# A long-convolution and feed-forward kernel on one core: one transform step, 32-row taps, one filter sum by accumulating transfers, and new orders

## The chip, the cores and the metric

The kernel runs on one core of a Trainium2 chip. The metric is the device time of one execution in microseconds, 258.08 us in the middle of three runs (257.58 to 259.14). All five engines of the core take part: TensorE (PE in the profile; its weight loads are PEld) multiplies, VectorE (DVE) and ScalarE (ACT) do elementwise work and empty PSUM, GpSimd (POOL) computes small powers and issues accumulating transfers, SyncE (SP) issues the other transfers.

## The reference

The reference has two halves. In the first, the layer-normed input q gates a long causal convolution: k is shifted by four taps, multiplied by v, convolved along the sequence (2048 tokens, 640 channels) with a filter as long as the sequence, and added to the input. The second is a gated feed-forward block on the layer-normed sum.

```python
k_shift = k_shift + k_pad[:, t:t + S, :] * shift_k[:, ks - 1 - t][None, None, :]   # t in range(4)
kv = k_shift * v
y = irfft(rfft(kv padded to 2S) * rfft(ssm_k padded to 2S))[:S] + kv * ssm_D
h = x + _layernorm(x) * y
h2 = h + (silu(_layernorm(h) @ w_gate) * (_layernorm(h) @ w_up)) @ w_down
```

## The kernel before

The sequence is cut into four blocks of 512 tokens. The convolution is done per block in a frequency space of 512 points: signal block j is transformed to XH (a "signal transform", xfwd), filter block m to a spectrum (kfwd), block i of the output is the sum over j of products of signal j with a combined filter C[i-j] (prod), and the inverse transform (inverse) gives block i back, followed by the residual, the second layer norm and the transposed store into hnT for the feed-forward step (ffn). The line `SEQ` fixes the order in which these steps enter the graph: signal block 1 (S1), products into output block 1 (P11), inverse 1 (I1), feed-forward of block 0 (F0) and so on.

Every operation is a task with a name, added by `g.add` with the engine it may run on and what it reads and writes. `PLAN` holds one hand-fixed order of task numbers per engine (pe, act, dve, pool, sp) and one string `units`, which gives each PSUM tile one of four units of two banks. Each engine runs its list strictly in order. `arrange` (L135) adds the waits: a task that opens a PSUM tile waits for the users of the tile that had that unit before. So an engine that has to wait holds back all that stands behind it in its list.

Names that the text uses: `ktM.P` transposes filter block M for the even or odd half, `kfM.fpc` transforms it (L588) and `kbM` are its sums and differences, `kteM.P` and `kfMe...` the copies out of PSUM; `kcM` or `kcomb(M)` adds neighbouring filter spectra (L677); `tpI.c` are the tap matmuls of block I from channel chunk c on (L738), `keI.c` their copies out of PSUM, `kvI.c` the multiplication by v (L745); `xfI...` the signal transform (L625 or L588), `xbI.n` its sums on VectorE; `pJI.ff` the products (L780); `ybI` and `ivI` the inverse; `fgI`, `fuI` gate and up matmuls (L1032), `muI` their product, `dnI` the down matmuls (L1118); `laI` the first layer norm.

The tap step (L722 to L747) is a set of small matmuls: for each chunk of 128 channels and each of 7 offsets, one matmul per group of 64 channels, with K = 64 rows and 256, 192, 128, 64, 192, 128 or 64 columns. It multiplies a shifted slice of k by a block-diagonal tap matrix. So a chunk takes 14 matmuls of 7 steps, two side by side on the two halves of the array, and a block's five chunks 70 matmuls in three tasks with a PSUM tile each.

The signal transform has three forms. `fulls` (L593) does all by matmuls. `halves` (L574) splits the tokens into even and odd, takes 8 groups of 4 matmuls of 320 columns, and adds and subtracts the halves on VectorE (two operations of 2560 elements per partition). `quads` (L611) splits twice, takes 8 groups of 2 matmuls, and needs four operations of 1280 and two of 2560 on VectorE. Before, blocks 1, 2 and 3 use `quads` (`R4X`). Filter transforms use `halves`.

`kcomb(2)` adds filter spectrum 2 onto spectrum 1 by one VectorE operation of 5120 elements (L687); `kcomb(3)` does it with two accumulating transfers that POOL issues (L680, `addto`, L570).

Of the kernel before, what the change touches and what calls it, by code (L numbers as in the profile page):

```python
# [12 lines left out]
P = 128  # L13
# [37 lines left out]
class _Graph:  # L51
# [41 lines left out]
    def add(self, name, engs, fn, kind, r=(), w=(), pr=(), pw=(), skip=(), dma=False):  # L93
# [4 lines left out]
        t.opens = None  # L98
# [18 lines left out]
        for pt in pw:  # L117
            if not pt.writers:
                t.opens = pt
# [15 lines left out]
    def arrange(self, plan):  # L135
# [19 lines left out]
        for t in self.order["pe"]:  # L155
            if t.opens is not None:
                prev = last.get(t.opens.unit)
                if prev is not None:
                    t.pre = {x for x in prev.users if x.eng != "pe"}
                    t.deps.update(t.pre)  # L160
                last[t.opens.unit] = t.opens
# [21 lines left out]
    def emit(self, block):  # L183
# [29 lines left out]
        for t in self.glob:  # L213
            kn = known[t.eng]
            fill = self.fills.get(t.name)
            if fill:
                wait_for(t, t.pre | {x for x in t.deps if x.name == fill[0]})
                prog["pe"].append(lambda e, t=t, fill=fill: self.filler(e, t.opens, *fill))
# [50 lines left out]
    "act":  # L269
# [10 lines left out]
    "dve":  # L280
# [10 lines left out]
    "pool":  # L291
        "19 17 15 16 125 165 174 158 192 183 223 225 224 342 396 362 281 371 285 401 380 289 406 389 343 293 420 415 527 466 "
        "470 561 474 552 478 579 570 684 586 591 529 705 710 698 637 732 723 641 645 750 649 741 "
        "",
    "sp":
        "0 2 3 8 4 6 10 7 230 9 11 13 14 235 296 226 12 229 297 227 481 231 167 176 228 234 295 233 194 185 482 232 364 282 373 "
        "290 391 294 286 382 480 653 652 471 563 554 467 475 479 581 572 651 734 725 638 752 646 743 642 650 798 807 801 804 "
        "810 "
        "",
    "units":  # L300
        "0131203132312001201201213230032110213023012230313133033220021021122013200230230222110332013110130232003210332301202110"
        "01310112312301210312031012210230131023033303012010313012013"
        "",
# [7 lines left out]
def bass_sequential_preLN__ssm_conv_h3__swiglu_ffn__prompt_kernel(  # L311
# [30 lines left out]
    SA = ()  # L342
    DA = ((1,2),(1,3),(2,3),(3,3))
    KD = (3,)
    DD = (2,)
    LO = (('k',2),('k',3),('x',3))
# [3 lines left out]
    JP = (0,1)  # L350
    SEQ = "P01 K W F0 S1 P11 I1 P02 P12 P03 P13 F1 S2 P22 I2 P23 F2 S3 P33 I3 F3"
# [5 lines left out]
    BNH = ()  # L357
# [4 lines left out]
    R4X = (1,2,3)  # L362
# [19 lines left out]
    with ExitStack() as es:  # L382
# [29 lines left out]
        KO = sb("KO", 143616, [2, 2, D])  # L412
# [246 lines left out]
        def kfwd(m, dst):  # L659
            if m in R4K:  # L660
                quads("kf%d" % m, KT[m], dst, KO, D ** 0.5 / N, m)
                return
# [3 lines left out]
            halves("kf%d" % m, KT[m], dst, KO, D ** 0.5 / N, m)  # L666
            if ("k", m) in LO:
                bfly("kb%d" % m, dst[:, 0:2], KO[:], dst[:, 0:2], dst[:, 2:4], 4 * D, part=1)
                addto("kb%d.1" % m, dst[:, 0:2], KO[:])
                return  # L670
            if ("k", m) in MB:
                bfly("kb%d" % m, dst[:, 0:2], KO[:], dst[:, 0:2], dst[:, 2:4], 4 * D)
                return
            for f in range(2):
                bfly("kb%d.%d" % (m, f), dst[:, f], KO[:, f], dst[:, f], dst[:, f + 2], 2 * D)

# [22 lines left out]
        def taps(i):  # L699
# [22 lines left out]
            for c0 in (0, 2, 4):  # L722
                nc_ = min(2, NC5 - c0)
                pt = g.tile()
# [504 lines left out]
```

## Time and profile before

| what | value |
|---|---|
| timed runs | 257.58, 258.08, 259.14 us; median 258.08 us |
| span of the profiled execution | 256.0 us (no other time is given for that execution) |
| median less span | 2.1 us |
| PE, DVE, ACT, POOL busy in the span | 97%, 78%, 72%, 23% |
| granted TensorE clock | 1.000 |

The span runs from the first to the last instruction. A matmul's end is modelled: its busy time includes the drain, so rows of 320-column matmuls show a mean of 300 ns, while a long run of them starts one every 136 ns. The cost of a matmul on PE is therefore read from the start of one group to the start of the next.

### The profile page before, as it was taken

How to read it: one execution, taken by the hardware profiler on the slowest of the kernel's cores; microseconds unless marked ns; L12 is line 12 of the kernel's file. 1: busy time of each engine (PE TensorE's matmuls, PEld its weight loads, DVE VectorE, ACT ScalarE, POOL GpSimd, SP SyncE). 2: the span in 40 equal slices, each digit the busy share in tenths (PEclk: the TensorE clock that was granted, in tenths of full speed). 3: DMA queues.
4: the chain of work that ended last, by engine and by line, in shares of the span. 5: the costliest groups of instructions: out<-in, count | busy, mean ns of one | idle time of the engine just before them, and what ended most of it. 6: DMA issues, size and time to landing. Idle time of an engine off the chain costs nothing.

```text
span 256.0 us, 5303 instructions
## 1 busy us (share of the span) xinstructions
PE 248.5 (97%) x2253; PEld 194.7 (76%) x2253; DVE 199.8 (78%) x256; ACT 184.6 (72%) x302; POOL 58.6 (23%) x56
## 2 busy tenths in 40 slices
PE   7999997999999999999999999999999999999995
PEld 4767773587888766888887766788886678888763
DVE  3698999999999999999999989999959534111142
ACT  2489999999996895587899789739981854526410
POOL 1001003082312053950030813334130314000000
PEclk9999999999999999999999999999999999999999
DMA  6999946787995049886956036497870142600011
GB/s 224 323 339 208 403 161 134 220 207 192 326 188 95 0 75 126 150 165 168 248 100 109 3 55 139 108 213 139 149 128 0 30 100 43 140 0 3 0 45 57
DMA packets 37620, 35.29 MB, mean 138 GB/s; under 512 B 21203, under 2 KB 32478, under 8 KB 37598
## 3 DMA queue, kind: packets, MB, share of 16 engines
q1 hardware_dynamic: 31792, 23.82, 33.2%
q0 software_dynamic: 5792, 11.14, 25.3%
q8 instruction: 17, 0.28, 0.4%
q14 instruction: 5, 0.04, 0.1%
q10 hardware_dynamic: 14, 0.01, 0.0%
HBM read 16.55 MB, written 2.62 MB: 75 GB/s over the span
## 4 chain that ended last, share of the span: by engine, by line
PE 59%; DVE 32%; DMA 4%; POOL 1%; SPq 1%; issue 1%; ACT 0%; DVEq 0%
PE ps L1032 32%; PE ps L1118 16%; DVE tt L780 9%; DVE Y L780 5%; DMA tab<-cst_tab 4%; PE ps L602 3%; PE ps L922 2%; DVE gu L1053 2%; DVE C L780 2%; DVE XH L637 2%; DVE C L564 2%; PE ps L995 2%; PE ps L622 2%; PE ps L584 2%; POOL mv L840 1%; SPq L450 1%
## 5 line engine op out<-in xcount | busy, mean ns | idle before, releaser
L1118 PE MATMUL ps<-Wd,gu 128*128 128x320 bf16 (+1 forms) x420 | 58.7, 300 | 0.0
L1118 PEld LDWEIGHTS ps<-Wd,gu 128*128 128x128 bf16 (+1 forms) x420 | 38.7, 97 | 18.4 <-issue 3.6
L780 DVE TENSOR_TENSOR tt<-XH,C 128x2560 bf16<-128x2560 bf16 (+1 forms) x31 | 47.8, 1572 | 0.6 <-ACT XH L458 0.6
L1053 DVE TENSOR_TENSOR gu<-gu,ub 128x1024 bf16<-128x1024 bf16 (+1 forms) x32 | 19.9, 621 | 26.4 <-ACT gu L1040 13.8
L1040 ACT ACTIVATE gu<-ps 128x1024 bf16<-128x1024 f32 (+1 forms) x32 | 29.4, 924 | 12.1 <-PE ps L1032 11.9
L1045 ACT ACTIVATE ub<-ps 128x1024 bf16<-128x1024 f32 x24 | 24.6, 1024 | 13.3 <-PE ps L1032 11.4
L1032 PE MATMUL ps<-hnT,GB 128*128 128x256 bf16 x280 | 34.0, 273 | 0.0
L1032 PE MATMUL ps<-hnT,UB 128*128 128x256 bf16 x280 | 33.8, 273 | 0.0
L1032 PEld LDWEIGHTS ps<-hnT,UB 128*128 128x128 bf16 x280 | 27.3, 98 | 3.4 <-ACT KO L458 0.2
L1032 PEld LDWEIGHTS ps<-hnT,GB 128*128 128x128 bf16 x280 | 27.2, 98 | 3.3
L1032 PE MATMUL ps<-hnT,GA 128*128 128x256 bf16 x240 | 28.8, 273 | 0.0
L1032 PE MATMUL ps<-hnT,UA 128*128 128x256 bf16 x240 | 28.5, 273 | 0.1
L840 POOL TENSOR_TENSOR mv<-mv,half 128x1 f32<-128x1 f32 x16 | 21.2, 1328 | 23.9 <-DVE mv L838 23.9
L1032 PEld LDWEIGHTS ps<-hnT,UA 128*128 128x128 bf16 x240 | 23.4, 98 | 3.4 <-ACT C L458 0.5
L1032 PEld LDWEIGHTS ps<-hnT,GA 128*128 128x128 bf16 x240 | 23.4, 98 | 3.2 <-DVE XH L461 0.3
L843 ACT ACTIVATE qo<-xh 128x640 bf16<-128x640 bf16 x28 | 21.0, 750 | 5.8 <-DMA xh<-in_A_q_dram 3.3
L584 PE MATMUL ps<-KT,tab 128*128 128x320 bf16 x128 | 19.8, 300 | 1.8 <-ACT K3r L458 0.7
L937 ACT ACTIVATE qo<-ps,one,st 128x640 bf16<-128x640 f32 x16 | 13.7, 887 | 9.8 <-PE ps L922 9.0
L571 POOL DMA_DIRECT2D xh<-RB x12 | 10.7, 889 | 34.4 <-DVE RB L1135 23.0
L584 PEld LDWEIGHTS ps<-KT,tab 128*128 128x128 bf16 x128 | 11.4, 98 | 8.6 <-ACT K3r L458 1.6
L840 POOL TENSOR_TENSOR st<-st,half 128x4 f32<-128x4 f32 x4 | 8.0, 1988 | 33.3 <-DVE st L835 21.5
L458 ACT ACTIVATE XH<-ps 128x640 bf16<-128x640 f32 x19 | 13.3, 736 | 1.4 <-PE ps L622 0.7
(112 smaller groups left out, 384.3 us busy)
## 6 DMA issues: line engine op xcount, KB each, us to landing
C<-US POOLq DMA_DIRECT2D x6, 640.0 KB, 6.0
kc<-in_A_ssm_k_dram SPq DMA_DIRECT2D x4, 640.0 KB, 10.3
xh<-in_A_q_dram SPq DMA_DIRECT2D x4, 640.0 KB, 5.6
out_dram<-xh SPq DMA_DIRECT2D x15, 160.0 KB, 1.9
kvo<-in_A_v_dram SPq DMA_DIRECT2D x3, 640.0 KB, 4.5
xh<-RB POOLq DMA_DIRECT2D x12, 160.0 KB, 2.9
Wd<-in_B_w_down_dram SPq DMA_DIRECT2D x1, 1280.0 KB, 7.9
C<-K3r POOLq DMA_DIRECT2D x2, 640.0 KB, 8.0
```

Source lines behind the costliest of these rows:

```text
L458: return e.activation(out=dst[1], in_=src(), func=ACTF.Copy, scale=scale)
L571: return g.add(name, "pool", lambda e, n: e.dma_start(dst, src, accum_op=ALU.add, max_dma_last_dim=4096), ("acc", 2 * int(np.prod(dst.shap ...
L584: last = e.matmul(pt.f(c, W), tab[:, f, cs, j], src[:, j, c * W:(c + 1) * W], start=(j == js[0]), stop=(j == js[1]))
L780: g.add(nm, "dve", lambda e, n_: e.tensor_tensor(out=d, in0=a, in1=b, op=op), ("sb", n * D), r=[a, b], w=[d])
L840: g.add(name + "r", "pool", lambda e, n: e.tensor_tensor(out=dst, in0=tmp, in1=hf, op=ALU.pow), ("pp", 4), r=[tmp, half[:]], w=[dst])
L843: g.add(name + "m", "act", lambda e, n: e.activation(out=junk, in_=x, func=ACTF.Identity, scale=-1.0 / D, accum_out=sm), ("aa", D, 0), r=[ ...
L937: g.add(nm + "e", "act", lambda e, n, pt=pt, q2=q2, s=s, j=j: e.activation(out=q2, in_=pt.f2(W), func=ACTF.Identity, scale=s[:, 3, j:j + 1 ...
L1032: last = e.matmul(pt.f(q // 2, 256, o=256 * (q % 2)), w[:, c, f0:f0 + P], hnT[:, c, cols], start=(c == 0), stop=(c == NC5 - 1))
L1040: g.add("sg%d.%d%d" % (i, h, gp), "act", lambda e, n, pa=pa, gv=gv, nf=nf: e.activation(out=gv, in_=pa.f(0, 256 * nf).rearrange("p (f x) - ...
L1045: g.add("su%d.%d%d" % (i, h, gp), "act", lambda e, n, pb=pb: e.activation(out=ub[:].rearrange("p b x -> p (b x)"), in_=pb.f(0, 1024), func ...
L1053: g.add("mu%d.%d%d" % (i, h, gp), "dve", lambda e, n, gv=gv, ubv=ubv: e.tensor_tensor(out=gv, in0=gv, in1=ubv, op=ALU.mult), ("sb", 256 * ...
L1118: last = e.matmul(pt.f(c, W), gu[k, fb, col(i, j)], Wd[k, fb, c * W:(c + 1) * W], start=st, stop=sp)
```

## The change

Four things change. `R4X` loses block 1, so signal block 1 is transformed by `halves` and not by `quads`. `KD` gains block 2, so `kcomb(2)` is two accumulating transfers. For blocks 1 to 3 the first four channel chunks of the taps form one task of 32-row matmuls, four side by side, which opens two PSUM tiles at once; the fifth chunk stays as it was. And all five orders and the PSUM units are new. `DV`, `KOT` and `BNT` are empty tuples, so the code that they guard adds no task; `KO` becomes four names for the same place.

```diff
-    KD = (3,)
+    KD = (2,3)
+    T32 = ((0, 4, 32), (4, 1, 64))
-    R4X = (1,2,3)
+    R4X = (2,3)
...
-            for c0 in (0, 2, 4):
-                nc_ = min(2, NC5 - c0)
-                pt = g.tile()
+            for c0, nc_, rr in T32 if i in KVACT else ((0, 2, 64), (2, 2, 64), (4, 1, 64)):
+                nr = P // rr
+                pts = [g.tile() for _ in range(nr // 2)]
...
                         for s in (0, 1, 2, 3, -1, -2, -3):
                             j0, j1 = max(0, s), min(3, 3 + s) + 1
                             k0 = 16 + s
-                            for r in range(2):
-                                rows = slice(64 * r, 64 * r + 64)
-                                last = e.matmul(pt.f(r, 64 * (j1 - j0), o=256 * b + 64 * j0), ks[rows, c, k0:k0 + 509:4], diag[rows, c, j0 - s:j1 - s, :],
-                                                start=(s == 0), stop=(s == -3))
+                            for r in range(nr):
+                                rows = slice(rr * r, rr * r + rr)
+                                x0 = rr * r % 64
+                                last = e.matmul(pts[r // 2].f(r % 2, rr * (j1 - j0), o=4 * rr * b + rr * j0), ks[rows, c, k0:k0 + 509:4],
+                                                diag[rows, c, j0 - s:j1 - s, x0:x0 + rr], start=(s == 0), stop=(s == -3),
+                                                **({"tile_position": (rr * r, 0)} if rr < 64 else {}))
...
+                    for h, pt in enumerate(pts):
+                        kh_ = kr[:, 2 * h:2 * h + 2]
+                        evac("ke%d.%d%s" % (i, c0, "ab"[h] if nr > 2 else ""), (kh_, kh_),
+                             lambda pt=pt, nc_=nc_, rr=rr: pt.f2(4 * rr * nc_).rearrange("p r (b y) -> p r b y", b=nc_), 8 * rr * nc_, pt)
+                    g.add("kv%d.%d" % (i, c0), "dve", lambda e, n, d=d, vv=vv, ks_=ks_, rr=rr, nr=nr: e.tensor_tensor(
+                        out=d.rearrange("p j (b x) -> p b j x", x=rr), in0=ks_.rearrange("p b (r j x) -> p (b r) j x", r=nr, j=4),
+                        in1=vv.rearrange("p j (b x) -> p b j x", x=rr), op=ALU.mult), ("sb", N * nc_), r=[vv, ks_], w=[d])
```

In `arrange`, `opens` becomes a list, since a tap task now opens two tiles and waits for the users of both. Per block of 1 to 3 the taps have two matmul tasks instead of three, still three copies out of PSUM (`ke.0a` and `ke.0b` of 1024 elements, `ke.4` of 512), and two multiplications by v (2048 and 512 elements) instead of three (1024, 1024, 512).

The task numbers in `PLAN` are not the same in both files, so the orders are told here by the names behind them. The parts that the prediction speaks of:

```
PE, before:  xf0(2) kf0(8) kt1 xf0(2) kt2.0 xf0.31 kt2.1 xf0(3) kf1 ... tp1.2 tp1.0 iv0.0 iv0.1 tp1.4 kf2/kf3/xf1 mixed ... fu0.00
             (first matmul of F0; xf1 last group, kt3.1 and seven groups of kf3 stand among F0)
PE, after:   xf0.00 kf0(8) xf0(3) kt1 xf0(4) kf1(5) kt2 kf1(3) kt3.0 tp1.0 tp1.4 iv0.0 iv0.1 kf2(5) kt3.1 kf2/xf1/kf3 mixed ... fg0.00
             (all of xf1 and four groups of kf3 ahead of F0)
PE, both:    ... F0 ... iv1, dn0, two groups of F1, taps of block 2, xf2, rest of F1, dn1, taps of block 3, iv2, xf3, F2, F3
DVE, after, new among the copies out of PSUM: kf0e.111 kte2.1 ke1.4 kf2e.001 kf2e.010 kte3.1 xf1e.001 (ACT before, but kf0e.111)
DVE, before, now on ACT or POOL: kf0e.011 kte0.0 lp0
DVE, before the last kv of block 2: p03.c mu1.00 kv2.2 kv2.0 kv2.4 p03.d ... iv1.3n
DVE, after:                         iv1.3n ... p03.c kv2.4 p03.d kv2.0 ... mu1.00
POOL, before: iv0.0r iv0.1r kb2.1 iv0.3r iv0.2r kb3.1 kc3.1 kc3.0 la1r
POOL, after:  iv0.0r iv0.1r lp0 kb2.1 kc2.1 iv0.2r iv0.3r kc2.0 kb3.1 kc3.1 kc3.0 lp1 la1r
SP, before:   kT1 GA itab UB v1 UA kT2 PKu ht0.0 ht0.1 GB WdC x1 WdB ht0.3 ht0.2 v2 WdA
SP, after:    kT1 itab UA v1 x1 GB PKu WdC GA UB WdB kT2 ht0.0 ht0.1 v2 ht0.2 ht0.3 WdA
```

More of the change, by code (lines that the diff above doesn't have):

```diff
@@ L97, in add @@
         t.pre = set()
-        t.opens = None
+        t.opens = []
         t.tiles = []
@@ L118, in add @@
             if not pt.writers:
-                t.opens = pt
+                t.opens.append(pt)
             else:
@@ L155, in arrange @@
         for t in self.order["pe"]:
-            if t.opens is not None:
-                prev = last.get(t.opens.unit)
+            for pt in t.opens:
+                prev = last.get(pt.unit)
                 if prev is not None:
-                    t.pre = {x for x in prev.users if x.eng != "pe"}
-                    t.deps.update(t.pre)
-                last[t.opens.unit] = t.opens
+                    t.pre |= {x for x in prev.users if x.eng != "pe"}
+                last[pt.unit] = pt
+            t.deps.update(t.pre)
         for t in self.tasks:
@@ L217, in emit @@
                 wait_for(t, t.pre | {x for x in t.deps if x.name == fill[0]})
-                prog["pe"].append(lambda e, t=t, fill=fill: self.filler(e, t.opens, *fill))
+                prog["pe"].append(lambda e, t=t, fill=fill: self.filler(e, t.opens[0], *fill))
             wait_for(t, t.deps)
@@ L356, in bass_sequential_preLN__ssm_conv_h3__swiglu_ffn__prompt_kernel @@
     BN = (0,)
-    BNH = ()
+    BNT = ()
+    KOT = ()
     DT = ()
@@ L411, in bass_sequential_preLN__ssm_conv_h3__swiglu_ffn__prompt_kernel @@
         v0 = sb("v0", 134400, [4, D])
-        KO = sb("KO", 143616, [2, 2, D])
+        KO = [sb("KO%d" % m, 174336 if m in KOT else 143616, [2, 2, D]) for m in range(4)]
         ub = sb("ub", 148736, [2, N])
@@ L742, in taps @@
                     ks_ = XT[i % 2][:, c0:c0 + nc_, :]
[L743 to L747 removed]
+                    kr = ks_.rearrange("p b (r y) -> p r b y", r=nr)
+                    for h, pt in enumerate(pts):
[5 more added lines that the diff above has]
+                        in1=vv.rearrange("p j (b x) -> p b j x", x=rr), op=ALU.mult), ("sb", N * nc_), r=[vv, ks_], w=[d])
                     continue
@@ L799, in prod @@
                 op2(nm + ".d", yim, u[:, :, 0], u[:, :, 1], ALU.add, 4)
+                return
+            if (j, i) in DV:
+                x, k, re = XH[j % 2][:], cm[:], tt[:, 1].rearrange("p a b d -> p (a b) d")
+                im = US[:].rearrange("p a b c d -> p (a b) c d")
+                ksw = bass.AP(k.tensor, k.offset + D, [list(k.ap[0]), [2 * D, 4], [-D, 2], [1, D]])
+                nm = "p%d%d" % (j, i)
+                for f2 in range(2):
+                    s = slice(f2, f2 + 3, 2)
+                    op2(nm + ".%da" % f2, t1, x[:, s], k[:, s], ALU.mult, 4)
+                    op2(nm + ".%dc" % f2, re[:, s], t1[:, :, odd], t1[:, :, 1 - odd], ALU.subtract, 2)
+                addto(nm + ".0e", y[:, :, odd], re)
+                op2(nm + ".0b", im, x, ksw, ALU.mult, 8)
+                for q in range(2):
+                    addto(nm + ".%df" % q, y[:, :, 1 - odd], im[:, :, q])
                 return
@@ L973, in inverse @@
                     stats(nm, x, q[:], m[:, 0:1], m[:, 1:2])
-                rstd(nm, m[:, 1:2], m[:, 3:4], m[:, 2:3], half[:, 0:1], i in BNH or i in SA, D ** -2.0 if i in SA else float(D))
+                rstd(nm, m[:, 1:2], m[:, 3:4], m[:, 2:3], half[:, 0:1], (i, j) in BNT or i in SA, D ** -2.0 if i in SA else float(D))
                 if i in NACT:
@@ L984, in inverse @@
                 g.add(nm + "n", "dve", lambda e, n, x=x, q=q, m=m, mm_=mm_: e.tensor_scalar(
-                    out=q[:], in0=x, scalar1=mm_, scalar2=m[:, 3:4], op0=ALU.subtract if i in BNH + SA else ALU.add, op1=ALU.mult),
+                    out=q[:], in0=x, scalar1=mm_, scalar2=m[:, 3:4], op0=ALU.subtract if (i, j) in BNT or i in SA else ALU.add, op1=ALU.mult),
                       ("ts", D), r=[x, mm_, m[:, 3:4]], w=[q[:]])
```

42 lines of the change are left out of this document (18 added, 24 removed), and 53 rows, old and new, of the table PLAN.

## The prediction

> **What bounds the kernel now.** I read the page first: the engine shares, then the slices.
>
> ```profile
> span 256.0 us, 5303 instructions
> PE 248.5 (97%) x2253; PEld 194.7 (76%) x2253; DVE 199.8 (78%) x256; ACT 184.6 (72%) x302; POOL 58.6 (23%) x56
> ...
> PE   7999997999999999999999999999999999999995
> ...
> DVE  3698999999999999999999989999959534111142
> ACT  2489999999996895587899789739981854526410
> ```
>
> PE is busy in nearly every slice. DVE is at nine tenths from the fifth slice to the twenty-fifth, ACT from the fourth to the eleventh. So two limits lie close together up to about 160 us, and PE alone remains after it. The table by stretches says how close (PE, PEld, DVE, ACT, POOL).
>
> ```profile
> core 0: us, PE busy (x) PEld busy (x) DVE busy (x) ACT busy (x) POOL busy (x), PEclk, DMA share, GB/s
> ...
> 28.20:40.50 12.30, 12.30 (x147) 9.08 (x144) 12.19 (x11) 12.30 (x21) 0.00 (x0) 1.00 0.73 245
> 40.50:49.30 8.80, 6.72 (x40) 2.81 (x40) 8.42 (x12) 8.80 (x16) 2.38 (x2) 1.00 0.56 119
> 49.30:113.20 63.90, 63.51 (x588) 51.27 (x588) 63.30 (x69) 53.60 (x92) 26.44 (x19) 1.00 0.74 161
> 113.20:161.30 48.10, 47.83 (x440) 37.39 (x440) 46.27 (x60) 41.77 (x72) 12.54 (x11) 1.00 0.53 116
> 161.30:253.40 92.10, 92.07 (x781) 74.80 (x780) 48.79 (x72) 49.43 (x81) 15.27 (x17) 1.00 0.39 78
> ```
>
> From 40.5 to 113.2 DVE works 71.72 of 72.7 us; from 161.3 on PE has 92.07 of 92.1. In 40.5 to 49.3 ACT is full (8.80 of 8.80) while PE runs only 40 matmuls. The chain of waits and PE's timeline price them (start, duration, what; a bracket holds idle time and what ended it).
>
> ```profile
> 18.68 1.12 PE ps L550 x20
> ...
> 24.18 3.27 PE ps L602 x24
> ...
> 121.58 13.10 PE ps L1032 x120
> ...
> 138.46 2.28 PE ps L734 x63
> 140.74 3.93 PE ps L1032 x35
> ```
>
> ```profile
> 14.72 3.96 PE L584 MATMUL ps<-KT,tab 128*128 128x320 bf16 x28 [0.20 <-DMA tab<-cst_tab]
> ...
> 43.29 0.45 PE L622 MATMUL ps<-kvo,tab 128*128 128x320 bf16 x2
> 43.88 0.44 PE L622 MATMUL ps<-kvo,tab 128*128 128x320 bf16 x2
> ...
> 105.78 2.35 PE L1032 MATMUL ps<-hnT,GA 128*128 128x256 bf16 x20
> 108.05 2.47 PE L734 MATMUL ps<-diag,kT 64*128 64x256 bf16 x70
> 110.45 2.36 PE L1032 MATMUL ps<-hnT,GB 128*128 128x256 bf16 x20
> 113.23 0.72 PE L622 MATMUL ps<-kvo,tab 128*128 128x320 bf16 x4 [0.42 <-DVE kvo L745]
> ...
> 159.69 1.69 PE L622 MATMUL ps<-kvo,tab 128*128 128x320 bf16 x10 [0.24 <-DVE mv L838]
> ```
>
> A 320-column matmul costs 3.27/24 = 0.136 us, so the 40 of that stretch are 5.45 us of work in 8.80: PE stands idle for 3.35 us there, waiting for ACT to empty PSUM. Two groups of the signal transform start 0.59 us apart (43.29, 43.88) for 0.27 us of matmuls. The next idle time is 0.42 us at 113.23, where signal block 2 waits for the product kv2 on DVE. Then come 0.24 us at 159.69 and, early, 0.20 us at 14.72 for a table. So PE's stalls that the change could reach are 3.35 + 0.42 + 0.24 + 0.20 = 4.2 us, and everything else is PE's own work.
>
> **The change, part by part.**
>
> *Signal block 1 by halves.* PE gets 8 groups of 4 matmuls for 8 of 2: 16 x 0.136 = +2.18 us. ACT's eight copies stay. It falls where PE waited on ACT, so part of it costs nothing as long as those stalls last; I count it in full against the removed stalls. DVE prices:
>
> ```profile
> L1053 DVE TENSOR_TENSOR gu<-gu,ub 128x1024 bf16<-128x1024 bf16 x24 | 16.5, 688 | 23.1 <-ACT gu L1040 13.8 <-ACT ub L1045 9.3
> ...
> L637 DVE TENSOR_TENSOR XH<-OS,XH 128x2560 bf16<-128x2560 bf16 x5 | 7.4, 1487 | 0.0
> L984 DVE TENSOR_SCALAR qo<-xh,mv 128x640 bf16<-128x640 bf16 x16 | 7.1, 444 | 2.7 <-POOL mv L840 2.7
> ...
> L637 DVE TENSOR_TENSOR OS<-XH,OS 128x1280 bf16<-128x1280 bf16 x6 | 4.9, 820 | 0.2 <-ACT OS L458 0.2
> ...
> L745 DVE TENSOR_TENSOR kvo<-XT,kvo 128x1024 bf16<-128x1024 bf16 x6 | 3.9, 685 | 0.0
> ...
> L687 DVE TENSOR_TENSOR C<-C,C 128x5120 bf16<-128x5120 bf16 x1 | 2.8, 2822 | 0.0
> ...
> L461 DVE TENSOR_SCALAR KO<-ps 128x640 bf16<-128x640 f32 x1 | 0.8, 825 | 0.4 <-PE ps L584 0.4
> ...
> L460 DVE COPY KT<-ps 128x1280 bf16<-128x1280 bf16 x1 | 0.8, 815 | 0.0
> ```
>
> The next start on DVE comes some 0.08 us before the modelled end (the operation at 50.65 below lasts 1.49 us and the next begins at 52.05), so an operation costs 0.08 us less than its duration. DVE loses four operations of 1280 elements and keeps two of 2560: 4 x 0.74 = -2.96 us.
>
> *Filter sum 2 by transfers.* DVE loses one operation of 5120 elements, 2.82 - 0.08: -2.74 us. POOL gets two issues and the queues two transfers of 640 KB.
>
> ```profile
> C<-K3r POOLq DMA_DIRECT2D x2, 640.0 KB, 8.0
> ...
> C<-KO POOLq DMA_DIRECT2D x1, 640.0 KB, 5.8
> ```
>
> ```profile
> 50.65 1.49 DVE L564 TENSOR_TENSOR C<-C,KO 128x2560 bf16<-128x2560 bf16 x1
> ...
> 83.08 1.49 DVE L780 TENSOR_TENSOR tt<-XH,C 128x2560 bf16<-128x2560 bf16 x1
> ```
>
> ```profile
> 52.45 1.39 POOL L571 DMA_DIRECT2D C<-KO  x1 [9.31 <-DVE C L564]
> ```
>
> ```profile
> 27.47 0.34 SPq L450 DMA_DIRECT2D kvo<-in_A_v_dram  x1
> ```
>
> The sum is needed by the first product of signal 0 with C[2], at 83.08. Its own filter is final on DVE at 50.65 + 1.49 = 52.1. Issue and landing one after another, 1.39 + 5.8 for the KO transfer and 1.39 + 8.0 for the half that waits for it, end near 69 us; 14 us of product work on DVE hide them. I take nothing; with that cover gone all lateness past 83 us would stand on DVE. Behind them on POOL stand the powers iv0.2r and iv0.3r, whose inputs DVE makes only after kb2.0, the last thing that the transfers ahead of them wait for; la1r stood behind the transfers of filter 3 before as well. On SP, GA moves behind v1 (issued at 27.47, when signal block 0 has been read), x1 and GB: with them 3.4 MB, by 245 GB/s of the stretch 28.2 to 40.5 some 14 us, near 42; F0 begins some 8 us later and the transform groups ahead of it hide it. UB is first used later, and kT2 only by the taps of block 2. I take nothing; with the cover gone it is the lateness of the last load, up to one more 8.0 us.
>
> *Taps in 32 rows.* The widths (front: 1024 columns per group of 64 channels and chunk) sum to 5 chunks x 2 x 1024 = 10240 columns a block. At 256 columns per 13.10/120 = 0.109 us one after another they would take 4.37 us; 2.28 us from start to the next start at 140.74 in the chain says that two run side by side (2.18 us, and 0.10 for 35 steps). With the change between full and half array the block costs 110.45 - 105.78 less the 2.18 us of 20 gate matmuls, 2.49 us. After: four chunks x 512 columns = 0.87, one chunk x 1024 = 0.44, 0.10 for 35 steps, 0.31 for three changes of array form as dear as the two now, and 0.11 if a 32-column step costs as much as a 64-column one (8 steps x 13.6 ns): 1.83 us, so -0.66 per block and -2.0 for three. No row shows a 32-row matmul. Best end: without the extra change and the floor, -0.87 each. Worst end: an issue limit, with weight loads and matmuls at the mean rate of now, 2.28/126 = 18 ns; 252 instructions give 4.6 us and 4.8 with the changes, +2.3 each. I take the middle row's rate since pairs plainly overlap. The task opens two PSUM units, so it waits for the users of both, and both copies must end before other groups get them.
>
> ```profile
> L458 ACT ACTIVATE XT<-ps 128x1024 bf16<-128x1024 f32 x6 | 6.1, 1064 | 0.1
> ```
>
> Where ACT is full that is no new wait, and elsewhere PE has two units left; I take nothing, bounded by one copy, 1.06 us a block.
>
> The multiplications by v become 2048 + 512 elements. From 1280 to 2560 elements DVE takes 1487 - 820 = 667 ns, 0.52 ns each, so 2048 take 0.685 + 0.53 = 1.22 us where two took 1.37, less 0.08: -0.07 us a block. If runs of 32 elements halved the rate it would be +1.2; I take -0.07, as runs of 64 show no loss (0.685 for 1024).
>
> *Orders.* Six copies out of PSUM go from ACT to DVE: kte2.1 and kte3.1 (0.82 each), kf2e twice, xf1e.001 (0.83 each) and ke1.4 (at most that): 4.96, less 6 x 0.08: +4.5 us on DVE, as much less on ACT, which lets PE run through 40.5 to 49.3. kte0.0 goes the other way, early. And the last groups of signal block 0 stand ahead of kt2.
>
> ```profile
> 28.28 2.90 DVE L780 TENSOR_TENSOR tt<-XH,C 128x2560 bf16<-128x2560 bf16 x2 [0.29 <-ACT XH L458]
> ```
>
> Here DVE waited for them. PE's work ahead of that point shrinks by kt2 (20 transposes, 1.12 us) and the table wait, with some 0.2 us of hidden ends: DVE's chain starts about 1.6 us sooner.
>
> *The sum up to signal block 2* (113.23 now). DVE: -1.6 for the start, -2.96 - 2.74 - 0.14, +4.5: -2.9. In the new order p03.d (2560 elements, 1.41 us) and iv1.3n (0.36) stand ahead of kv2 and mu1.00 (0.61) behind: +1.2. Together -1.8, to 111.4. PE alone: -0.42 - 3.35 - 0.20 + 2.18 - 2 x 0.66 = -3.1, to 110.1. DVE is later, so the gain there is 1.8 us. *Behind it* the 1.2 us come back to DVE (-2.9 by inverse 2), so PE decides: tap block 3 gives -0.66, and the stall at 159.69 gives -0.3, as the groups of signal block 3 now stand among inverse 2, dn1.3 and fg2.00. F2 and F3 are PE's work unchanged. The sum is -1.8 - 0.66 - 0.3 = -2.8: a span of 253.2.
>
> The timed median lies 2.1 us above the span; I keep that: **255.3 us**.
>
> **The rivals.**
>
> *All of PE's stalls go.* For it: ACT is relieved by 4.5 us of copies against 3.35 us of stall. Against: DVE gets these copies and is as full. PE's account: -4.2 + 2.18 - 2.0 = -4.0: 254.1 us, and 253.4 with the best price of the taps.
>
> *The gain on DVE is eaten.* The copies now stand in DVE's strict order among products, so PE waits for DVE where it waited for ACT, and the earlier start is lost at the next wait. Then DVE gains -2.96 - 2.74 - 0.14 + 4.5 + 1.2 = -0.1 by signal block 2, and PE 0.66 behind it: -0.8: 257.3 us. For it: 71.72 of 72.7 us.
>
> *32-row matmuls are limited by issue.* This ends on the other side. The block costs 4.8 us; PE's account up to signal block 2 is 110.1 + 2 x 3.0 = 116.1, +2.9, block 3 adds 2.3 and the late stall gives 0.3: +4.9, 263.0 us. It turns slower than now when a block takes over 3.2 us. For it: no row has so dense a stream. Against: pairs run together.
>
> *Each small matmul pays a floor.* With 27 ns (64 columns at 0.109/256) for each of 112 matmuls, one after another, the block is 3.0 + 0.44 + 0.4 = 3.9 us; PE is at 110.1 + 4.1 = 114.2 at signal block 2 (+1.0), and +1.4 - 0.3 behind: 260.2 us. Against: 70 matmuls in 2.28 us have only 33 ns each while their widths average 146 columns, 62 ns; so they overlap, and a floor is paid per step. The Trainium skill, "TensorEngine Tiling (Array Packing)", section "Instruction Overhead", speaks for this rival: about 60 cycles for each matmul, and no tiling from a dimension that is small already; here the widths fall to 32 to 128 columns. By that rule, taken per matmul, the taps would cost more than now; the trace does not bear it out for two tiles and shows nothing for four.
>
> *The accumulations land late.* The transfers share their engines with the weight loads (8.0 us for 640 KB already). If landing took double, C[2] would be ready near 83 us and each further us would hold DVE; two more eat what DVE gained: 258 us.
>
> **How the numbers follow.** Forecast 0.43, all stalls go 0.13, eaten 0.22, issue limit 0.13, floor 0.05, late transfers 0.04. A measurement of this kernel can tell about 1% from no change, so faster means below 255.5 us and slower above 260.7. The forecast's own range is 254.2 to 256.4; 0.33 of the 0.43 lies below 255.5, 0.10 above. Faster: 0.33 + 0.13 = 0.46. Slower: the issue limit, 0.13. Same: 0.10 + 0.22 + 0.05 + 0.04 = 0.41. The range 253.2 to 260.5 leaves out the issue limit and a little below.
>
> **What would show it.** Taps: the groups of 32-row matmuls, some 1.8 us per block from the matmul before to the one after, and four starts close together. Halves: 32 matmuls for signal block 1, no 1280-element operations of it. Filter sum: no 5120-element addition, two more transfers landed well before the first product with C[2]. Stall: PE's idle time near 40 to 50 us well under 3.35 us. Signal block 2's first matmul near 111 us. I am wrong if the tap block takes over 2.5 us, if PE's idle time in that stretch merely moves to waits on DVE's copies, or if DVE's first product of block 0 starts no sooner than now.

## The result, and the profile after

| | before | after |
|---|---|---|
| median of the timed runs | 258.42 us (22 runs, 257.26 to 260.11) | 261.07 us (22 runs, 257.76 to 268.11) |
| ratio after to before, 95% interval | | 1.0066 [1.0041, 1.0090] |
| profiled execution | span 256.0 us | 261.59 us, span 259.7 us |

The forecast was 255.3 us, with a span of 253.2 us. The runs after scatter far more than those before. The ratio leaves out the eight longest executions after (261.99 us and more, granted clock 0.981 to 0.987), and since the kernel's own idle time lowers that clock (*warm*, below), it may understate the loss a little: the plain medians stand at 261.07 / 258.42 = 1.010.

The page of the profile after, beside the one shown of before:

```profile
span 259.7 us, 5661 instructions
...
PE 249.5 (96%) x2437; PEld 196.0 (75%) x2437; DVE 194.3 (75%) x248; ACT 184.6 (71%) x301; POOL 59.9 (23%) x59
...
PE   7999999849999999999999999999999999999995
...
DVE  2699999994699999999999987799978422121232
...
PEclk9999999988999999999999999999999999999999
```

DVE does 5.5 us less (199.8 before). PE has one gap, in the eighth and ninth slices, and the granted clock falls behind it. The table by stretches (PE, PEld, DVE, ACT, POOL, then PEclk, DMA share, GB/s) and PE's timeline show the gap from near.

```profile
40.50:50.70 10.20, 10.20 (x75) 6.75 (x73) 10.20 (x13) 10.20 (x19) 4.42 (x5) 1.00 0.98 202
50.70:55.80 5.10, 0.33 (x4) 0.04 (x2) 5.10 (x5) 4.04 (x10) 3.40 (x2) 1.00 1.06 178
55.80:60.70 4.90, 4.90 (x30) 3.69 (x31) 4.90 (x6) 0.95 (x1) 2.28 (x2) 0.65 1.12 234
```

```profile
50.31 0.71 PE L581 MATMUL ps<-kvo,tab 128*128 128x320 bf16 x4
55.79 5.10 PE L1049 MATMUL ps<-hnT,GA 128*128 128x256 bf16 x30 [4.77 <-issue]
```

The 3.35 us of stalls between 40.5 and 49.3 are gone: PE is busy for all of 40.5 to 50.7. But then F0's first gate matmul (fg0.00) starts at 55.79, after 4.77 us of idle time. It reads the columns of hnT that the first two transposed stores, ht0.0 and ht0.1, fill. And its group of 30 takes 5.10 us at a granted clock of 0.65, where 3.44 us are usual (below): 1.66 more. Both together are 6.4 us, and 259.7 - 6.4 = 253.3.

Here are the issues on SP and on POOL in that stretch (start, duration of the issue), and after them the time from issue to landing of single transfers (the last number): first those issued at 45.83 and 46.53, then those at 47.16 and 47.44.

```profile
40.44 0.37 SPq L447 DMA_DIRECT2D Wd<-in_B_w_down_dram  x1
40.85 4.94 SPq L450 DMA_TRANSPOSE kT<-in_A_k_dram  x1
45.83 1.28 SPq L450 DMA_TRANSPOSE hnT<-qo  x1
47.16 1.28 SPq L450 DMA_TRANSPOSE hnT<-qo  x1
```

```profile
46.53 1.41 POOL L568 DMA_DIRECT2D C<-KO  x1 [0.27 <-DVE C L561]
47.44 1.75 POOL L568 DMA_DIRECT2D C<-C  x1
```

```profile
C<-KO POOLq DMA_DIRECT2D x1, 640.0 KB, 9.0
hnT<-qo SPq DMA_TRANSPOSE x1, 2.7
```

```profile
C<-C POOLq DMA_DIRECT2D x1, 640.0 KB, 12.9
hnT<-qo SPq DMA_TRANSPOSE x1, 8.5
```

ht0.0 lands at 45.83 + 2.7 = 48.5. ht0.1, issued 0.63 us after C<-KO, lands at 47.16 + 8.5 = 55.7, just after C<-KO (46.53 + 9.0 = 55.5), and fg0.00 starts 0.1 us later. The profile writes "issue" beside the idle time, since it found no releaser; the landing is the one that fits. In the kernel before both stores took 2.6 us, and C<-KO was issued long after them, at 52.45. Its issues of kT2 and of the two stores, and their landing:

```profile
37.19 2.77 SPq L453 DMA_TRANSPOSE kT<-in_A_k_dram  x1
...
43.13 2.96 SPq L453 DMA_TRANSPOSE hnT<-qo  x2
```

```profile
hnT<-qo SPq DMA_TRANSPOSE x2, 2.6
```

The other steps of the change are seen in the timelines of PE and DVE:

```profile
111.03 1.88 PE L732 MATMUL ps<-diag,kT 32*128 32x128 bf16 x126
...
117.49 0.71 PE L619 MATMUL ps<-kvo,tab 128*128 128x320 bf16 x4
...
140.62 1.30 PE L732 MATMUL ps<-diag,kT 32*128 32x128 bf16 x112
```

```profile
26.98 1.49 DVE L783 TENSOR_TENSOR tt<-XH,C 128x2560 bf16<-128x2560 bf16 x1 [0.15 <-ACT XH L455]
```

A tap block takes 1.88 us (2.47 before). DVE's first product of that group starts at 26.98 (28.28 before). Signal block 2's first matmul starts at 117.49; less the 6.4 us it would be 111.1.

### The profile page after: what moved, and what is told of

Read it like the earlier page. It is cut to its first block, busy times and chain, and to the rows that moved or that the text cites. A ratio compares the mean times of both kernels' runs of the same rounds, so it can differ in the third digit from the quotient of the medians.

```text
span 259.7 us, 5661 instructions
## 1 busy us (share of the span) xinstructions
PE 249.5 (96%) x2437; PEld 196.0 (75%) x2437; DVE 194.3 (75%) x248; ACT 184.6 (71%) x301; POOL 59.9 (23%) x59
## 4 chain that ended last, share of the span: by engine, by line
PE 83%; ACT 8%; DMA 5%; DVE 1%; issue 1%; SPq 0%
PE ps L1049 45%; PE ps L1135 19%; PE ps L581 4%; PE ps L599 3%; DMA xh<-RB 3%; PE ps L944 3%; PE ps L732 2%; PE ps L939 2%; PE ps L1012 2%; DMA k0n<-in_A_k_dram 2%; PE ps L619 1%; ACT qo L862 1%; ACT qo L860 1%; PE ps L547 1%; ACT qo L954 1%; ACT RB L1151 1%
## 5 line engine op out<-in xcount | busy, mean ns | idle before, releaser
L1135 PEld LDWEIGHTS ps<-Wd,gu 128*128 128x128 bf16 (+1 forms) x420 | 38.8, 97 | 18.3 <-issue 3.5
L1049 PE MATMUL ps<-hnT,GA 128*128 128x256 bf16 x240 | 30.2, 282 | 5.0 <-issue 4.8
L1049 PEld LDWEIGHTS ps<-hnT,GA 128*128 128x128 bf16 x240 | 24.0, 101 | 9.5 <-ACT qo L862 5.1
L857 POOL TENSOR_TENSOR mv<-mv,half 128x1 f32<-128x1 f32 x16 | 19.2, 1204 | 50.7 <-DVE mv L855 50.6
L568 POOL DMA_DIRECT2D xh<-RB x12 | 11.8, 981 | 53.0 <-ACT RB L1151 53.0
L1151 ACT ACTIVATE RB<-ps,st 128x640 bf16<-128x640 f32 x11 | 8.7, 791 | 11.4 <-DMA xh<-RB 7.6
L581 PEld LDWEIGHTS ps<-KT,tab 128*128 128x128 bf16 x128 | 12.1, 98 | 5.5 <-ACT C L455 0.4
L455 ACT ACTIVATE XH<-ps 128x640 bf16<-128x640 f32 x17 | 11.9, 715 | 3.7 <-PE ps L619 2.4
```

The source lines that it names most:

```text
L455: return e.activation(out=dst[1], in_=src(), func=ACTF.Copy, scale=scale)
L568: return g.add(name, "pool", lambda e, n: e.dma_start(dst, src, accum_op=ALU.add, max_dma_last_dim=4096), ("acc", 2 * int(np.prod(dst.shap ...
L581: last = e.matmul(pt.f(c, W), tab[:, f, cs, j], src[:, j, c * W:(c + 1) * W], start=(j == js[0]), stop=(j == js[1]))
L857: g.add(name + "r", "pool", lambda e, n: e.tensor_tensor(out=dst, in0=tmp, in1=hf, op=ALU.pow), ("pp", 4), r=[tmp, half[:]], w=[dst])
L1049: last = e.matmul(pt.f(q // 2, 256, o=256 * (q % 2)), w[:, c, f0:f0 + P], hnT[:, c, cols], start=(c == 0), stop=(c == NC5 - 1))
L1135: last = e.matmul(pt.f(c, W), gu[k, fb, col(i, j)], Wd[k, fb, c * W:(c + 1) * W], start=st, stop=sp)
```

## The experiments

Two questions were asked in turn: what makes ht0.1 late, and whether the forecast's own terms are right once it is not. Orders are given by the names of the front part; a number in a diff is a place in `PLAN`.

### Where the store is held: late_both, late_second, kt2_behind, warm

*late_both* makes the two transfers wait for the store.

```diff
+    "lates": {"kb2.1": "ht0.1"},
...
+        for name, other in PLAN.get("lates", {}).items():
+            byname[name].deps.add(byname[other])
```

> The changed kernel, with one dependency more: the accumulating transfer kb2.1 (and so kc2.1 behind it on POOL) waits for the transposed store ht0.1. Theory A (collision: the two accumulating transfers issued at 46.5 and 47.4 us hold back ht0.1, issued at 47.2 and landed at 55.7): ht0.1 lands within 3 us of its issue, PE's 4.9 us of idle time ahead of fg0.00 shrinks to under 1 us, the clock stays at 1.000, and the time is 259.7 - 4.9 - 1.8 = 253.0 us of span, some 255 us. Theory B (ht0.1 is late because the load kT2 was put ahead of it on SP): no change, a span near 259 us, and idle time of 4 to 5 us.

Measured: 257.56 us, ratio to before 0.9969 [0.9930, 1.0009], span 255.8. ht0.1 lands 2.7 us after its issue and the idle time ahead of fg0.00 is gone, so the place of the transfers is what made it. Not all of the 6.4 us come back, for the later transfers now hold others. ACT's timeline:

```profile
59.00 2.49 ACT L429 ACTIVATE KO<-ps 128x640 bf16<-128x640 f32 x4 [0.87 <-DMA C<-KO]
...
75.38 1.02 ACT L1031 ACTIVATE gu<-ps 128x1024 bf16<-128x1024 f32 x1 [2.00 <-DMA K3r<-KO]
```

KO is scratch of both filters and lies on rows of gu, so copies into either wait until the transfers have read KO.

*late_second* makes only the second transfer wait (`"lates": {"kc2.1": "ht0.1"}`).

> The changed kernel, with only kc2.1 (the transfer that the change added) waiting for ht0.1; kb2.1 keeps its place at 46.5 us. Theory A with the second transfer as the cause: like late_both, a span near 253 us. Theory A with the early place of the first as the cause: ht0.1 still lands some 5 to 6 us after its issue, 2 to 3 us of idle time, a span near 256 us. Theory B: no change, near 259 us.

Measured: 260.21 us, 1.0065 [1.0025, 1.0104], span 257.9. ht0.1 needs 6.5 us, and fg0.00 starts at 53.78 behind 3.18 us of idle time. C<-KO alone, which is no part of filter sum 2, holds the store.

*kt2_behind* moves the transposed load kT2 behind ht0.1 on SP.

```diff
-... GA UB WdB kT2 ht0.0 ht0.1 v2
+... GA UB WdB ht0.0 ht0.1 kT2 v2
```

> The changed kernel, with the load kT2 put behind ht0.1 on SP. Theory A: the stores are issued up to 1 us sooner, but ht0.1 still meets both accumulating transfers; 3 to 5 us of idle time stay, a span of 257 to 260 us. Theory B: ht0.1 lands within 3 us, no idle time, a span near 253 us.

Measured: 266.91 us, 1.0324 [1.0277, 1.0370], span 265.6. Neither theory foresaw it. The first two stores land in 2.6 and 3.5 us and PE has no idle time at 50. But kT2 (12.8 us) now meets the transfers, and the stores of the second half, ht0.2 and ht0.3, take 15.2 and 18.3 us:

```profile
77.07 2.29 PE L1020 MATMUL ps<-hnT,GA 128*128 128x256 bf16 x10 [10.79 <-DMA hnT<-qo]
```

*warm* puts 20 filler matmuls of 512 columns, work that the reference doesn't have, into PE's idle time, which prices the half clock.

```diff
     "fills": {
+        "fg0.00": ["zmem", 20],
```

> The changed kernel, with 20 matmuls of 512 columns on constant data put into the PSUM tile of fg0.00 ahead of its wait for the store; they compute nothing that is used. If the half-speed matmuls after the idle time (17 at 0.213 instead of 0.109 us) are a consequence of the idle time, the clock stays at 1.000, the wait ends when it did, and the span is some 1.8 us shorter, near 258 us. If the clock falls for another reason, it falls here too and the span stays near 260 us.

Measured: 259.71 us, 1.0041 [1.0004, 1.0078], span 258.1. The store is as late as ever (fg0.00 at 55.40), but the group of 30 runs at full clock:

```profile
50.65 4.48 PE L473 MATMUL ps<-gu 128*128 128x512 bf16 x20
55.40 3.45 PE L1020 MATMUL ps<-hnT,GA 128*128 128x256 bf16 x30 [0.27 <-DMA hnT<-qo]
```

5.10 - 3.45 = 1.65 us of the loss are the clock after the idle time, and the span falls by 1.6. The profile names the store here, since the wait for it is seen alone. The Trainium skill, "TensorE: Matmul & The Clock Gate", Part 1, says that the array falls to half clock after about 3.4 us of idleness; the granted clock of 0.65 in the stretch after 4.77 us of it agrees. Here somewhat less was enough: by the profile's idle times the clock fell to 0.65 behind 3.02 us as well (plain_first, 54.7 to 59.6 us) and stayed at 1.00 behind 2.85 us (ko3, 103.5 to 107).

### Which transfer holds which: ko3, plain_first, before_xfer

*ko3* is late_both with filter 3's KO at the place of kT (block 1's signal step enters the graph ahead of filter 3 for that), and kT2 behind WdA.

```diff
-    KOT = ()
+    KOT = (3,)
-    SEQ = "P01 K W F0 S1 P11
+    SEQ = "P01 S1 K W F0 P11
```

> The changed kernel with the two first accumulating transfers of filter sum 2 made to wait for the second transposed store (as in late_both), and in addition filter 3's scratch moved from KO to the place of the transposed keys kT, so that neither ACT's copies of filter 3 nor the silu copies into gu wait for an accumulating transfer to have read KO; the load kT2 goes behind WdA for that. Theory A (what is left of late_both over the forecast are the stalls of 0.89 us at 58.7 and 1.36 us at 75.0, both made by KO): both go, span 255.8 - 2.25 = 253.6 us, time 255.5 us or 0.988 of before. Theory B (the transfers are late whatever waits for them, and the next user waits in their place: DVE for C[2], or the taps of block 2 for the late kT2): the stalls come back as waits of PE for DVE or of DVE for C, and the span stays at 255 to 256.

Measured: 265.76 us, 1.0261 [1.0184, 1.0339], span 263.3. Theory A fell, theory B's mechanism came, much dearer. The two stalls by KO are gone, but kT2 and the last half of filter sum 3, issued 0.3 us apart near 71.3, both need some 19 us, and DVE waits:

```profile
C<-K3r POOLq DMA_DIRECT2D x1, 640.0 KB, 18.8
kT<-in_A_k_dram SPq DMA_TRANSPOSE x1, 19.7
```

```profile
90.35 2.82 DVE L757 TENSOR_TENSOR Y<-XH,C 128x5120 bf16<-128x5120 bf16 x1 [9.16 <-DMA C<-K3r]
```

In the kernel after, kT2 takes 7.1 us. So kT2 beside the accumulating transfers is bad in two places, and this kernel doesn't answer what freeing KO alone is worth.

*plain_first* is the changed kernel with plain copies for the two transfers; it leaves two additions out.

```diff
-e.dma_start(dst, src, accum_op=ALU.add, max_dma_last_dim=4096)
+e.dma_start(dst, src) if name in ("kb2.1", "kc2.1") else e.dma_start(dst, src, accum_op=ALU.add, max_dma_last_dim=4096)
```

> The changed kernel, but the transfers C<-KO and the first C<-C of filter sum 2 are plain copies on the same queue of POOL, of the same size, at the same place in the order: two additions are left out. Theory A1 (what holds the transposed store behind them is that they accumulate): the store issued near 47.2 lands within some 3 us, PE's idle time of 4.9 us ahead of F0's first gate matmul goes, and the time is some 6.7 us less than the changed kernel's, near 255. Theory A2 (it is their size and place: any transfer of 640 KB just ahead of the store holds it): the store still lands with the first transfer, near 53 to 55, idle time 3 to 5 us, time 258 to 261.

Measured: 259.83 us, 1.0068 [1.0030, 1.0106], span 259.1. The copies land sooner, in 4.3 and 6.0 us, and yet both stores are late, and PE is idle for 3.02 us:

```profile
C<-KO POOLq DMA_DIRECT2D x1, 640.0 KB, 4.3
C<-C POOLq DMA_DIRECT2D x1, 640.0 KB, 6.0
hnT<-qo SPq DMA_TRANSPOSE x2, 6.0
```

Theory A1 falls. That they accumulate is not needed; 640 KB ahead of the store are enough. (ht0.1 lands 0.1 us before PE goes on.)

*before_xfer* is the kernel before with filter sum 2 alone by transfers.

```diff
-    KD = (3,)
+    KD = (2,3)
 POOL:
-kb2.1 iv0.3r iv0.2r kb3.1
+kb2.1 kc2.1 iv0.3r iv0.2r kc2.0 kb3.1
```

> The kernel before with filter sum 2 alone changed: the DVE addition of 5120 elements gives way to two accumulating transfers, issued behind the transfer C<-KO that is there already. All other orders as before, so that the transfers start near 52.5, behind the stores that F0's first matmuls need. Theory A (the transfers hurt only where a transposed store stands behind them): DVE gains 2.74 us by the first product with C[2]; no new idle time of PE ahead of F0's first gate matmul; 0 to 2.7 us faster than before, 256 to 258. Theory B (the added traffic itself costs): later stores, loads and KO's readers land later, PE waits more than DVE gains, and the time is 259 or more.

Measured: 263.94 us, 1.0223 [1.0154, 1.0291], span 261.9. Theory B in size, theory A in kind. The first two stores (43.0, 44.8) are ahead of the transfers and land in 2.6 us. But ht0.2 and ht0.3 (59.3, 61.1) stand behind them, and take 8.5 and 9.4 us:

```profile
70.58 2.29 PE L997 MATMUL ps<-hnT,GA 128*128 128x256 bf16 x10 [4.90 <-DMA hnT<-qo]
```

My expectation had looked only at the first pair of stores. One part of the change, put into the old order, costs 2.2%.

### The one place that decides: sum_dve, kt2_ahead, best2, sum_dve_ahead

*kt2_ahead* swaps two loads on SP, nothing else (476 is kT2, 234 WdB).

```diff
-227 230 234 476 167 176 477
+227 230 476 234 167 176 477
```

> The changed kernel with the transposed load kT2 issued ahead of WdB on SP instead of behind it; nothing else. WdB waits for filter 3's transposes to near 40, and kT2 stands behind it with an issue of 4.9 us that ends at 45.8, so that the first two stores start at 45.8 and 47.2. With it ahead they start near 44.7 and 46.4, the second just ahead of C<-KO's issue at 46.5. Theory A (only a store that starts behind a transfer of 640 KB is held by it): the second store lands by 50, no idle time ahead of F0's first gate matmul, span 253 to 255.5, time 255 to 257.5. Theory B (the transfers hold the next transposed transfers instead, the stores of the second half at 57 to 59 behind the second C<-C): idle time of 3 us or more near 65, span 257 or more.

Measured: 255.38 us (254.63 to 255.43), ratio to before 0.9893 [0.9872, 0.9915], span 253.6. Theory A by its span, its time and the idle time; but the second store starts just behind C<-KO's issue, not ahead of it, and is in time all the same. SP's and POOL's issues, the store issued at 46.63, and PE:

```profile
34.35 7.91 SPq L421 DMA_TRANSPOSE kT<-in_A_k_dram  x1
42.31 0.59 SPq L418 DMA_DIRECT2D Wd<-in_B_w_down_dram  x1
44.87 2.96 SPq L421 DMA_TRANSPOSE hnT<-qo  x2
...
46.56 1.41 POOL L539 DMA_DIRECT2D C<-KO  x1 [0.27 <-DVE C L532]
```

```profile
hnT<-qo SPq DMA_TRANSPOSE x1, 3.4
```

```profile
50.34 0.71 PE L552 MATMUL ps<-kvo,tab 128*128 128x320 bf16 x4
50.88 3.44 PE L1020 MATMUL ps<-hnT,GA 128*128 128x256 bf16 x30
```

ht0.1 starts at 46.63 instead of 47.16. Measured from C<-KO's issue that is 0.07 us instead of 0.63, and it lands in 3.4 us instead of 8.5. Half a microsecond on SP is worth 259.7 - 253.6 = 6.1 us.

Why so little decides is seen in the counts of packets, the pieces in which the DMA engines move a transfer. From 49.5 to 52.5 us, first in the kernel after, then in kt2_ahead (q0 is POOL's queue, q1 SP's; packets, MB, share of the engines' time):

```profile
q0 software_dynamic: 157, 0.40, 96.2%
q1 hardware_dynamic: 177, 0.05, 22.3%
```

```profile
q0 software_dynamic: 244, 0.58, 109.2%
q1 hardware_dynamic: 8, 0.00, 0.4%
```

In the kernel after, the store's packets (256 bytes each, 640 in a store) and the transfer's (2560 bytes) take turns about one for one, so the store goes at the pace of the large packets; in plain_first it is 103 of SP's queue and 104 of POOL's from 49.0 to 50.5. Until then it is fast: kt2_ahead's queue of SP moves 577 packets in the 0.8 us from 48.0 to 48.8. In both kernels C<-KO's first packets move near 48.8, some 2.3 us after the start of its issue. kt2_ahead's store is through by then but for 10 packets, that of the kernel after still has 439 to go.

A rival falls with the traces: that the swap helps because kT2 is no longer under way beside the store. In sum_dve (below) kT2 lands at 48.75, ht0.0 starts 0.16 us behind C<-KO's issue, and lands in 3.5 us all the same. And in before_xfer two stores are held with no transposed load near them.

*best2* adds to it the second half of filter sum 2 behind K3r<-KO on POOL (197 is kc2.0, 224 kb3.1).

```diff
-183 192 197 224 226 225
+183 192 224 197 226 225
```

> As kt2_ahead, and the second half of filter sum 2 (C<-C for the first two planes) issued behind K3r<-KO instead of ahead of it, so that the stores of the second half at 57 to 59 and K3r<-KO have fewer bytes ahead of them. Theory A (order against the transposed stores is all that matters): stores of the second half land within 4 us, K3r<-KO within 8, no idle time of PE over 1 us behind 45 us, span 252.5 to 254, time 254.5 to 256. Theory B: C[2] gets ready too late for DVE's first product with it (near 80), which then waits, and PE behind it: span 255 or more.

Measured: 254.88 us (254.40 to 255.28), ratio to before 0.9880 [0.9857, 0.9902], span 252.5. Theory A by its numbers. ht0.2 and ht0.3 land in 3.4 us (5.0 in kt2_ahead), K3r<-KO in 6.7 (9.4). This is faster than both kernels of the case. That the edit gains over kt2_ahead isn't shown: of the 1.1 us of span between the two, 0.94 are there at the first matmul of the signal transform (10.98 and 11.92 us), where both kernels still have the same order.

*sum_dve* is the changed kernel with filter sum 2 on DVE again (`KD = (3,)`, the addition ahead of kb3.0, kc2.1 and kc2.0 gone), *sum_dve_ahead* is kt2_ahead with the same edit.

> The changed kernel with filter sum 2 alone undone: one addition of 5120 elements on DVE again, ahead of filter 3's difference, and no transfer C<-C. The transfer C<-KO stays at its early place (near 46.5, just ahead of the second transposed store). Theory A (the store is held by whatever transfer of 640 KB stands just ahead of it, and C<-KO alone is enough): PE still stands idle some 3 us ahead of F0's first gate matmul, the store landing with C<-KO near 53; what follows is lighter by two transfers; span 256 to 258, time 258 to 260. Theory B (filter sum 2 alone makes the loss): the idle time is under 1 us and the span 253 to 255.

> kt2_ahead with filter sum 2 on DVE, so without transfers C<-C. Theory A: no store stands behind a transfer of 640 KB, no idle time of PE over 1 us in 45 to 80; DVE is 2.74 us more loaded, of which some lies in its idle time near 61 to 67: span 253 to 255, time 255 to 257. If DVE's 2.74 us all show by signal block 2: 256, time 258.

Measured: sum_dve 259.70 us, 1.0071 [1.0041, 1.0101], span 259.0; sum_dve_ahead 257.97 us, 0.9995 [0.9979, 1.0011], span 255.8. In the first the store is still held, by C<-KO alone: it starts at 48.0 and lands in 6.2 us, 0.1 us before PE goes on, although the profile names a copy of ACT (theory A, with 1 us more of span than expected):

```profile
54.32 5.89 PE L1020 MATMUL ps<-hnT,GA 128*128 128x256 bf16 x27 [3.30 <-ACT OS L426]
```

In the second PE is idle for over 1 us only once (1.08, at 72.34, for a copy of ACT into gu), and 2.2 of DVE's 2.74 us show. So the four spans are a table of two by two:

| span, us | sum 2 by transfers | sum 2 on DVE |
|---|---|---|
| kT2 behind WdB | 259.7 | 259.0 |
| kT2 ahead of WdB | 253.6 | 255.8 |

Filter sum 2 by transfers is worth 2.2 us where the stores are ahead of them (255.38 against 257.97 us in time). Where they are not, it gains nothing: the 0.7 us between those two spans are within the scatter of the runs, and the ratios to before are 1.0066 and 1.0071.

### The forecast's other terms: taps64 and quads1, on best2

```diff
-    T32 = ((0, 4, 32), (4, 1, 64))
+    T32 = ((0, 2, 64), (2, 2, 64), (4, 1, 64))
```

> best2 with the taps of blocks 1 to 3 in 64 rows again, as in the kernel before; nothing else. Theory A (the forecast's term: 0.66 us per block, all three on PE's path): span 252.5 + 2.0 = 254.5 us, time 256.9. Theory B (DVE sets the end up to signal block 2, so that blocks 1 and 2 are hidden and block 3 alone shows): +0.7, time 255.6. Theory C (32-row matmuls pay a floor and gain nothing): no change or less, 254.9 or below.

Measured: 257.70 us, 0.9964 [0.9931, 0.9998], span 255.9, so 3.4 us of span more than best2. The tap blocks of 64 rows on PE:

```profile
105.44 2.47 PE L703 MATMUL ps<-diag,kT 64*128 64x256 bf16 x70
...
136.20 1.99 PE L703 MATMUL ps<-diag,kT 64*128 64x256 bf16 x56
```

Blocks 1 and 2 take 0.59 us less by 32 rows (2.47 to 1.88), block 3 0.69 (1.99 to 1.30): 1.87 us. The rest of the 3.4 are waits, such as 0.62 us for DVE's kv2 ahead of signal block 2, and 0.2 us of a later first signal matmul (11.17 us). Theory A, with some more than it says; B and C fall.

```diff
-    R4X = (2,3)
+    R4X = (1,2,3)
```

> best2 with signal block 1's transform split twice again (8 groups of 2 matmuls, four operations of 1280 and two of 2560 elements on DVE), the groups in the order of the kernel before at the places of the halves' groups, the four smaller operations among the products as their groups end; nothing else. Theory A (as forecast, DVE is later than PE up to signal block 2): the 2.96 us come back on DVE and show as waits of PE for DVE or ACT; PE's 2.18 us are not gained: span 252.5 + 1 to 3, time 256 to 258. Theory B (PE sets the end there as well, and the halves cost their matmuls): span 252.5 - 2.2 = 250.3, time 252.7.

Measured: 258.80 us, 1.0016 [0.9984, 1.0048], span 256.8: 4.3 more than best2, although PE has 2.18 us less to do. Theory A in kind, its size above what I gave. PE waits among xf1's groups again (busy for 7.98 of 8.80 us between 40.5 and 49.3), and ahead of signal block 2. The table of quads1 up to there, and the row:

```profile
49.30:114.00 64.70, 61.99 (x626) 49.15 (x626) 64.10 (x68) 50.20 (x87) 28.04 (x19) 1.00 0.70 138
```

```profile
114.04 0.72 PE L590 MATMUL ps<-kvo,tab 128*128 128x320 bf16 x4 [0.79 <-DVE kvo L719]
```

DVE is full (64.10 of 64.70) while PE has 2.7 us to spare, so DVE decides there. Of the 4.3 us, 1.0 are there at the first signal matmul already (11.97 us, 10.98 in best2), where the order is the same; and the smaller operations may stand in better places. So 3.3 us is an upper bound for what the halves are worth.

## Why the prediction was wrong

**The step that failed** is one sentence: "UB is first used later, and kT2 only by the taps of block 2. I take nothing". It asked who uses the load that is moved, and not who stands behind it on its queue. In the new order of SP kT2 follows WdB, which waits to 40.44, and its issue holds SP from 40.85 to 45.79; behind it stand ht0.0 and ht0.1. So ht0.1, issued 7.6 us ahead of C<-KO in the kernel before (44.90 and 52.45), falls to 0.63 us behind it. There its packets meet those of C<-KO. kt2_ahead shows that this place is the loss: the swap alone gives 253.6 us of span, where 253.2 were forecast, and 255.38 us of time, where 255.3 were.

**The filter sum's cover.** "14 us of product work on DVE hide them" was right for C[2], which nobody waits for here, but the working gave the transfers no effect on other transfers: 640 packets of a store that take turns with theirs. The rival "the accumulations land late" had the right resource, put it at C[2], and got 0.04. That C<-KO itself comes 6 us sooner in the new order (46.53, not 52.45), was nowhere in the working; late_second and sum_dve show that it is enough to hold the store. The gain of -2.74 us on DVE is 2.2 us of span (sum_dve_ahead against kt2_ahead).

**The half clock** was in no term: 1.65 us of the loss (warm).

**The terms that held**, with kT2 moved or by the rows after: the stall of 3.35 us on ACT is gone. The taps were to take 1.83 us per block and take 1.88; the term of -0.66 is -0.59, -0.59 and -0.69. Both rivals on the taps fall: with 4 tiles 112 matmuls go in 1.30 us, 11.6 ns each. The Trainium skill, "TensorEngine Tiling (Array Packing)", "Instruction Overhead", would have some 60 cycles for each, an estimate of 2.8 us for 112 at 2.4 GHz; its "TensorE: Matmul & The Clock Gate", Part 3, has the tiles overlap, and the trace agrees with that one. DVE's chain was to start 1.6 us sooner and starts 28.28 - 26.98 = 1.3 sooner.

**A number that came for another reason.** Signal block 2's first matmul was put at 111.4, with DVE last and PE's own work done at 110.1. In kt2_ahead it starts at 111.18, but without a wait, and kv2 on DVE has ended at 109.52 + 1.22 = 110.74:

```profile
109.52 1.22 DVE L719 TENSOR_TENSOR kvo<-XT,kvo 128x2048 bf16<-128x2048 bf16 x1
```

```profile
111.18 0.71 PE L590 MATMUL ps<-kvo,tab 128*128 128x320 bf16 x4
```

So PE comes last by 0.4 us there, 1.1 us later than worked out, and the agreement is partly luck. With quads DVE does decide up to there, as forecast (quads1); with halves the two are level. Behind it the forecast has 253.2 - 111.4 = 141.8 us, kt2_ahead 253.6 - 111.18 = 142.4 and the kernel before 142.8: 0.4 us gained there, not 1.0.

**What stays open.** The last packet of data of the held store moves at 53.1 us in the kernel after, and its landing is noted at 55.7; what fills these 2.6 us is not shown (1.15 us in kt2_ahead). What makes a load and a transfer take 19 us in ko3, beyond the turns of their packets, was not worked out. And how late the store is differs from run to run: the shortest two of the 22 took 257.76 and 258.05 us, and no trace shows them.

## What to carry to other kernels

Of an instruction that moves on a queue, ask first what then stands behind it, and only then who uses its result. Where small urgent transfers and large patient ones are issued within a microsecond of each other, put the small ones first by their order in the queues and look at issue to landing of each, not at the median of the group. A store of 160 KB is not small if it has 640 packets that wait their turn. A part of a change can lose in the old order (2.2% here) and gain 2.2 us in a fitting one, so undo it in both before judging it.

## What the runs showed of the hardware

A transposed store that takes 2.6 us alone took 6.5 us behind one accumulating transfer of 640 KB (late_second), 8.5 with a second one issued 0.3 us after the store (the kernel after), and 15.2 and 18.3 us in kt2_behind, where four such transfers were issued between 47.4 and 63.9 us. A transposed load and an accumulating transfer issued 0.3 us apart took 19.7 and 18.8 us (ko3), where the load takes 7.1 us in the kernel after. The Trainium skill, "DMA: Bandwidth & Descriptors", "Queues, rings and completion order", has each DMA engine take turns between queues packet by packet. The trace agrees: where both were under way, packets of the store and of the transfer went about one for one (177 and 157 in the kernel after, 103 and 104 in plain_first), and with 256 against 2560 bytes a packet (5120 in plain_first) that holds the store back and not the transfer. An accumulating transfer's first packets moved some 2.3 us after its issue began (48.8, issued at 46.53 and 46.56), a plain copy's 1.3 us (plain_first). Idle time of 4.77 us on PE cost 1.65 us more by the clock.
